# A linear attention with a mixture of four attention experts on one core: the gate logits are folded into the attention's matmul, PSUM tiles take two banks, and k^T v is computed per head on 64 columns of the array

## The chip, the cores and the metric

One core of a Trainium2 chip runs the whole program. The metric is the device time of one execution in microseconds (us), the median of several runs.

## The reference, cut to what matters

Eight batches (b) of eight heads (h), 576 tokens (s), head dimension 64; then four experts of head dimension 64 on the 512 values of each token, of which the two with the highest gate logits count.

```python
kv = np.einsum('bhsd,bhse->bhde', k, v)
out = np.einsum('bhsd,bhde->bhse', q, kv)
rms = np.sqrt(np.mean(out * out, axis=-1, keepdims=True) + 1e-06)
x = out / rms * g_norm            # then (B, S, 512)
logits = x @ w_gate               # top 2 of 4, softmax over these two
for e in range(E):
    q = x @ wq[e]
    k = x @ wk[e]
    v = x @ wv[e]
    scores = scale * (q @ k.transpose(0, 2, 1))   # causal
    a = softmax(scores)
    out += gate[e] * (a @ v @ wo[e])
```

## The kernel before

The 576 tokens are cut into five blocks (four of 128, one of 64). The program has two parts for each batch, written as Python generators. `attention` transposes q on TensorE (p_qT, L97 by way of a helper), computes k^T v for a pair of heads at a time (p_kv, L177) and keeps the two diagonal 64x64 squares of the 128x128 result (L186, L187). Then, block by block, it multiplies (p_out, L212), squares on ScalarE (sq, L220), sums on VectorE (sumsq, L222), adds eps (msq, L229), takes the power -0.5 on GpSimd (rstd, L238), scales (x_tok, L245), transposes (p_xT) and copies the result twice (xT as float32, L202, and xT_r in fp32r, L203).

`moe_block` begins with the gate logits: p_lt (L266) has four columns of weights and runs over all 576 tokens in float32, ScalarE copies it, TensorE turns it back (p_log), and VectorE makes the gate from it. Then come the values p_v (L322), the output of the batch before (`moe_final`: p_y L455, y_sb L463, output transfer L464), and for each of two pairs of experts: projections p_proj (L346, cast to qTp and kTp at L358), scores p_sc (L371, first all strips of one expert, then of the other) with an Exp (PT, L378) and a causal mask on GpSimd (L384) each, p_O (L409) with the row sums in a 65th column, its scaling on VectorE (O_sc, L418), and the transpose p_OT.

A float32 matmul leaves two records in the trace, one in fp32r or bfloat16 leaves one: p_kv has 4 pairs x 5 blocks = 20 matmuls a batch and 40 records.

While one batch is in `moe_block`, steps of the next batch's `attention` are put between its steps at a fixed ratio (`run_interleaved`). A scheduler then sets the order on each engine; the engines work off their own order without overtaking, and wait for one another by semaphores. PSUM is one pool of eight one-bank tiles. SP issues all transfers: the weights first, then q, k and v of batch 0 and 1, block by block in turn, in pieces of 256 bytes; the loads of batch b+2 are issued when batch b begins.

## Time and profile before

| | |
|---|---|
| median of 3 runs | 517.08 us (516.87 to 517.32) |
| span of the profiled execution, first to last instruction | 515.2 us |
| that span beside the median | 1.9 us shorter |
| TensorE busy, records | 400.2 us, 2472 |
| VectorE, ScalarE, GpSimd busy | 197.3, 173.9, 124.2 us |
| mean granted TensorE clock | 0.838 |

The profile gives no time of its own for the profiled execution besides the span; what lies around the span is taken as its distance from the median. Matmuls are pipelined and a record's own length is longer than its distance to the next, so costs are read from rows that span several records. The granted clock has two levels, 2.4 GHz (1.00) and 1.2 GHz (0.50); a mean between them says how much of a stretch ran at which.

### The profile page before, as it was taken

How to read it: one execution, taken by the hardware profiler on the slowest of the kernel's cores; microseconds unless marked ns; L12 is line 12 of the kernel's file. 1: busy time of each engine (PE TensorE's matmuls, PEld its weight loads, DVE VectorE, ACT ScalarE, POOL GpSimd, SP SyncE). 2: the span in 40 equal slices, each digit the busy share in tenths (PEclk: the TensorE clock that was granted, in tenths of full speed). 3: DMA queues.
4: the chain of work that ended last, by engine and by line, in shares of the span. 5: the costliest groups of instructions: out<-in, count | busy, mean ns of one | idle time of the engine just before them, and what ended most of it. 6: DMA issues, size and time to landing. Idle time of an engine off the chain costs nothing.

```text
span 515.2 us, 7111 instructions
## 1 busy us (share of the span) xinstructions
PE 400.2 (78%) x2472; PEld 285.5 (55%) x2472; DVE 197.3 (38%) x717; ACT 173.9 (34%) x569; POOL 124.2 (24%) x234
## 2 busy tenths in 40 slices
PE   0066696959969899679968799679968799679884
PEld 0055285726758467554757368454757367564661
DVE  1104334354252342543443442543433542543523
ACT  0013143611514215252246215251245215251440
POOL 3004202430132302351043302351043302340220
PEclk9999799869955599797988699796988699796866
DMA  8999908801390015900295014900200011000202
GB/s 168 206 195 204 206 13 160 118 1 42 108 205 15 2 41 128 199 2 0 92 182 96 1 41 119 207 3 0 87 7 1 1 42 52 0 2 1 93 0 92
DMA packets 125107, 40.31 MB, mean 78 GB/s; under 512 B 120208, under 2 KB 120208, under 8 KB 125072
## 3 DMA queue, kind: packets, MB, share of 16 engines
q1 hardware_dynamic: 125072, 39.87, 38.8%
q8 instruction: 19, 0.31, 0.3%
q14 instruction: 16, 0.13, 0.1%
HBM read 30.42 MB, written 9.44 MB: 77 GB/s over the span
## 4 chain that ended last, share of the span: by engine, by line
PE 56%; DVE 13%; POOL 11%; ACT 8%; issue 5%; DMA 3%; SPq 3%; POOLq 0%; DVEq 0%; ACTq 0%
POOL rstd L238 11%; PE p_kv L177 10%; PE p_lt L266 9%; PE p_proj L346 9%; PE p_out L212 5%; PE p_v L322 4%; PE p_qT L97 4%; DVE O_sc L418 4%; PE p_O L409 4%; PE p_y L455 3%; DVE x_tok L245 3%; PE p_sc L371 3%; ACT PT L378 3%; DVE sumsq L222 3%; ACT sq L220 2%
## 5 line engine op out<-in xcount | busy, mean ns | idle before, releaser
L384 POOL TENSOR_SCALAR_AFFINE_SELECT PT<-PT 128x128 bf16<-128x128 bf16 (+1 forms) x160 | 44.0, 290 | 195.4 <-ACT PT L378 191.0
L238 POOL TENSOR_TENSOR rstd<-msq,neg_half 128x8 f32<-128x8 f32 (+1 forms) x40 | 65.8, 1645 | 102.3 <-DVE msq L229 98.8
L378 ACT ACTIVATE PT<-p_sc 128x64 bf16<-128x64 f32 (+5 forms) x288 | 65.1, 341 | 14.5 <-PE p_sc L371 13.8
L409 PE MATMUL p_O<-vext,PT 128*128 128x65 bf16 (+2 forms) x480 | 43.5, 232 | 22.0 <-DVE x_tok L245 20.3
L371 PE MATMUL p_sc<-qTp,kTp 64*128 64x64 f32 (+5 forms) x288 | 49.3, 305 | 6.7 <-ACT kTp L358 4.2
L212 PE MATMUL p_out<-kv_all,qT_all 128*128 128x128 f32 (+1 forms) x320 | 52.8, 318 | 2.1 <-ACT PT L378 2.1
L245 DVE TENSOR_TENSOR x_tok<-p_out,rstd 128x512 f32<-128x512 f32 (+1 forms) x40 | 27.6, 689 | 65.3 <-POOL rstd L238 65.3
L177 PE MATMUL p_kv<-v_b,k_b 128*128 128x128 f32 (+1 forms) x320 | 51.7, 300 | 0.0
L97 PE MATMUL p_OT<-ident_b,O_sc 128*128 128x128 bf16 (+1 forms) x80 | 21.8, 273 | 38.4 <-DVE O_sc L418 38.1
L97 PE MATMUL p_qT<-ident_f,q_b 128*128 128x128 f32 (+1 forms) x160 | 28.6, 288 | 29.1 <-DMA q_b<-in_q_dram 29.1
L266 PE MATMUL p_lt<-xT,wg_f 128*4 128x64 f32 (+1 forms) x128 | 50.9, 564 | 0.0
L418 DVE TENSOR_SCALAR O_sc<-p_O,invr,gate 128x64 bf16<-128x64 f32 (+1 forms) x160 | 49.8, 334 | 1.6 <-PE p_OT L97 0.6
L409 PEld LDWEIGHTS <-PT 128*128 128x128 bf16 (+2 forms) x480 | 31.8, 124 | 30.8 <-POOL PT L384 11.1
L371 PEld LDWEIGHTS p_sc<-qTp,kTp 64*128 64x128 f32 (+1 forms) x288 | 39.3, 188 | 16.0 <-ACT kTp L358 5.8
L212 PEld LDWEIGHTS p_out<-kv_all,qT_all 128*128 128x128 f32 (+1 forms) x320 | 44.8, 209 | 5.8 <-ACT PT L378 3.5
L220 ACT ACTIVATE sq<-p_out 128x512 f32<-128x512 f32 (+1 forms) x40 | 23.8, 596 | 66.4 <-PE p_out L212 58.9
L222 DVE TENSOR_REDUCE sumsq<-sq 128x8 f32<-128x512 f32 (+1 forms) x40 | 27.2, 680 | 47.8 <-ACT sq L220 47.8
L177 PEld LDWEIGHTS p_kv<-v_b,k_b 128*128 128x128 f32 (+1 forms) x320 | 41.5, 194 | 6.3 <-issue 0.2
L174 ACT COPY qT_all<-p_qT 128x512 f32<-128x512 f32 x64 | 23.0, 419 | 61.5 <-PE p_qT L97 61.5
L186 DVE COPY kv_all<-p_kv 64x64 f32<-64x64 f32 x32 | 6.9, 216 | 90.1 <-PE p_kv L177 87.3
L97 PEld LDWEIGHTS p_qT<-ident_f,q_b 128*128 128x128 f32 (+1 forms) x160 | 19.4, 143 | 37.4 <-DMA q_b<-in_q_dram 19.9
L97 PE MATMUL p_xT<-ident_f,x_tok 128*128 128x128 f32 (+1 forms) x160 | 30.8, 330 | 8.7 <-DVE x_tok L245 5.8
(53 smaller groups left out, 419.9 us busy)
## 6 DMA issues: line engine op xcount, KB each, us to landing
q_b<-in_q_dram SPq DMA_DIRECT2D x32, 256.0 KB, 5.0
k_b<-in_k_dram SPq DMA_DIRECT2D x32, 256.0 KB, 5.0
v_b<-in_v_dram SPq DMA_DIRECT2D x32, 256.0 KB, 5.1
out_dram<-y_sb SPq DMA_DIRECT2D x32, 256.0 KB, 2.1
q_b<-in_q_dram SPq DMA_DIRECT2D x8, 128.0 KB, 5.1
k_b<-in_k_dram SPq DMA_DIRECT2D x8, 128.0 KB, 4.8
v_b<-in_v_dram SPq DMA_DIRECT2D x8, 128.0 KB, 4.4
out_dram<-y_sb SPq DMA_DIRECT2D x8, 128.0 KB, 2.3
```

The lines of the kernel that those rows point to most:

```text
L97: nc.tensor.transpose(out_ap, in_ap, ident[:npart, :npart])
L177: nc.tensor.matmul(p_kv[:, :], lhsT=kb[:nt, i, 2 * hp : 2 * hp + 2, :].rearrange("p h d -> p (h d)"), rhs=vb[:nt, i, 2 * hp : 2 * hp + 2, ...
L212: nc.tensor.matmul(p_out[:nt, hp * P : (hp + 1) * P], lhsT=qT2_all[:, hp, t0 : t0 + nt], rhs=kv2_all[:, hp, :], start=True, stop=True,)
L238: nc.gpsimd.tensor_tensor(out=rstd[:nt, :], in0=msq[:nt, :], in1=neg_half[:nt, :], op=AluOpType.pow,)
L245: nc.vector.tensor_tensor(out=x_tok[:nt, :].rearrange("p (h d) -> p h d", h=H), in0=p_out[:nt, :].rearrange("p (h d) -> p h d", h=H), in1= ...
L266: nc.tensor.matmul(p_lt[:, :], lhsT=wg_f[:, c, :], rhs=xT_sb[:, c, slo:shi], start=(c == 0), stop=(c == NCH - 1),)
L346: nc.tensor.matmul(p_proj[:, :], lhsT=wsrc[:, c, 2 * pr : 2 * pr + 2, :].rearrange("p e f -> p (e f)"), rhs=xT_r[:, c, plo:phi], start=(c ...
L371: nc.tensor.matmul(p_sc[:nk, :], lhsT=kT_pair[pb : pb + Hd, t0 : t0 + nk], rhs=qT_pair[pb : pb + Hd, lo:hi], start=True, stop=True,)
L378: nc.scalar.activation(PT[:nk, off + (lo - t0) : off + (hi - t0)], p_sc[:nk, :], ACTF.Exp, scale=scale,)
L384: nc.gpsimd.affine_select(out=PT[:nk, off : off + nk], in_=PT[:nk, off : off + nk], compare_op=AluOpType.is_ge, fill=0.0, base=0, pattern= ...
L409: nc.tensor.matmul(p_O[:nq, :], lhsT=PT[:nkk, col : col + nq], rhs=v_ext[:nkk, kbi, e, :], start=(kbi == 0), stop=(kbi == qci),)
L418: nc.vector.tensor_scalar(out=O_sc[:nq, el, :], in0=p_O[:nq, 0:Hd], scalar1=invr[:nq], scalar2=gate[:nq, qci, e : e + 1], op0=AluOpType.mu ...
```

## The change

It is a new text for nearly the whole kernel. What it does:

- The gate weights (scaled by g_norm) are multiplied with k^T v: per pair of heads one transpose (p_kt) and one matmul of 8 columns (p_kg), and the result stands as four more columns behind each head's 64 in kvx. p_out so gives the gate logits of each head unscaled; VectorE scales them with rstd (gl) and sums over heads (lg8). p_lt, its copies and p_log are gone, and so is the float32 copy of xT.
- k^T v is computed per head: 64 columns of weights, output on partitions 0 to 63 or 64 to 127, the two heads of a pair in turn. k and v come as 512 tokens with four in a row on one partition (1 KB runs); the remaining 64 tokens stand in tiles that are padded with zeros to 128 partitions. q comes as before.
- PSUM has three tiles of two banks (p_proj, p_sc, p_O, p_out) and two tiles of one bank (everything else).
- Projections are cut into 288 + 288 tokens. The scores of the two experts of a pair alternate, one bank each, and one Exp and one mask take both.
- p_O's reciprocal and scaling take three blocks and two experts at once; y is copied by ScalarE instead of VectorE; four y tiles instead of two.
- eps is a 65th column of sq, so msq is gone; q's copy moves from ScalarE to VectorE.
- Loads of batch 0 stand ahead of the weights, those of batch 1 behind them, with k and v ahead of q.
- `weave` puts the next batch's `stage1` between the steps of `stage2` by costs written beside each yield. `stage2` has both projections and scores first, then the output of the batch before, then both p_O.

```diff
...
+        step = 2 if fine else H
+        for h0 in range(0, H, step):
+            main(kt, k, h0, h0 + step)
+            main(vt, v, h0, h0 + step)
+            if h0 == 0:
+                rem(kr[b % 2], k)
+                rem(vr[b % 2], v)
+        for i, (t0, nt) in enumerate(blocks):
+            nc.sync.dma_start(
+                qt[:nt, i, :, :], q[b, :, t0 : t0 + nt, :].rearrange("h p d -> p h d")
+            )
...
+    def big(name):
+        return ps2.tile([P, 2, 512], FP32, tag="big", name=name)
+
+    def small(shape, name, dtype=FP32):
+        return ps1.tile(shape, dtype, tag="small", name=name)
...
+    loads = {0: load_qkv(0, fine=True)}
...
+    loads[1] = load_qkv(1)
...
+    def kv_pair(p_kv, c, kb, vb, krem, vrem):
+        for j in range(NF + 1):
+            for hh in range(2):
+                h = 2 * c + hh
+                lk, rv = (kb[:, h, j, :], vb[:, h, j, :]) if j < NF else (krem[:, h, :], vrem[:, h, :])
+                nc.tensor.matmul(
+                    p_kv[hh * Dh : (hh + 1) * Dh, c, :], lhsT=lk, rhs=rv,
+                    start=(j == 0), stop=(j == NF), skip_group_check=True,
+                )
+
+    def kv_copy(p_kv, kvb, kv2):
+        for hh in range(2):
+            pp = slice(hh * Dh, (hh + 1) * Dh)
+            nc.vector.tensor_copy(out=kvb[pp, :, hh, 0:Dh], in_=p_kv[pp, :, :])
+            nc.scalar.copy(kv2[pp, :, hh * Dh : (hh + 1) * Dh], p_kv[pp, :, :])
...
+        yield 4.3
...
+        p_kg = small([P, NCH, 2, E], "p_kg")
+        for c in range(NCH):
+            nc.tensor.matmul(
+                p_kg[:, c, :, :].rearrange("p a e -> p (a e)"),
+                lhsT=kt_sb[:, c, :],
+                rhs=wg_bd[:, c, :, :].rearrange("p a e -> p (a e)"),
+                start=True,
+                stop=True,
+            )
+        nc.vector.tensor_copy(out=kvb[:, :, :, Dh:GW], in_=p_kg[:])
...
+            p_o = big("p_out")
             for c in range(NCH):
...
+                    p_o[:nt, c // 2, (c % 2) * 2 * GW : (c % 2 + 1) * 2 * GW],
+                    lhsT=qT[:, c, t0 : t0 + nt],
+                    rhs=kvb[:, c, :, :].rearrange("p a g -> p (a g)"),
+                    start=True,
+                    stop=True,
+                )
+            po = p_o[:nt, :, 0 : 4 * GW].rearrange("p k (h g) -> p k h g", g=GW)
+            sq = sqs[i % 3]
+            nc.scalar.activation(
+                sq[:nt, :, 0:Dh].rearrange("p (k h) d -> p k h d", k=2),
+                po[:, :, :, 0:Dh],
+                ACTF.Square,
+                scale=1.0 / (Dh**0.5),
+            )
...
+            ms = blk.tile([P, H], FP32, tag="ms", name="ms")
+            nc.vector.tensor_reduce(ms[:nt], sq[:nt], axis=AX_X, op=AluOpType.add)
...
+            gl = blk.tile([P, H, E], FP32, tag="gl", name="gl")
+            nc.vector.tensor_tensor(
+                out=gl[:nt].rearrange("p (k h) e -> p k h e", k=2),
+                in0=po[:, :, :, Dh:GW],
+                in1=rb.to_broadcast([nt, 2, 4, E]),
+                op=AluOpType.mult,
+            )
+            nc.vector.tensor_reduce(
+                lg8[:nt, i, 0:E],
+                gl[:nt].rearrange("p h e -> p e h"),
+                axis=AX_X,
+                op=AluOpType.add,
+            )
...
+            if len(pend) > 1:
+                x_flush()
+                yield 0.45
...
+        def proj(pr):
+            out_t = []
+            for nm in ("q", "k"):
+                p_p = big("p_proj")
+                for c in range(NCH):
+                    for s in range(2):
...
+                nc.scalar.copy(
+                    t[:, 0:S].rearrange("p (s n) -> p s n", s=2), p_p[:, :, 0:HALF]
+                )
...
+            def piece(parts):
+                p_s = big("p_sc")
+                o = 0
+                for kb, lo, hi in parts:
+                    for el in range(2):
+                        pb = slice(el * Hd, (el + 1) * Hd)
...
+                            p_s[:, el, o : o + hi - lo],
...
+                    o += hi - lo
+                kb, lo, hi = parts[0]
+                d0 = strip_off[kb] + lo - kb * P
+                nc.scalar.activation(PT[:, :, d0 : d0 + o], p_s[:, :, 0:o], ACTF.Exp, scale=scale)
...
+            PT = res["PT", pr]
+            p_O = big("p_O")
...
+            groups = ((0, (0, 1, 2)), (1, (3, 4)))
+            for bank, qcs in groups:
...
+                    iv = inv[:nq, sub[0] : sub[0] + nn, :]
...
+                    nc.vector.tensor_tensor(
+                        out=osc[:nq, sub[0] : sub[0] + nn, :, :].rearrange("p n e f -> p (n e) f"),
+                        in0=po[:, :, 0:Hd],
+                        in1=iv.rearrange("p n e -> p (n e)").unsqueeze(2).to_broadcast([nq, 2 * nn, Hd]),
+                        op=AluOpType.mult,
...
+        yield from proj(0)
+        yield from scores(0)
+        yield from proj(1)
+        yield from scores(1)
+        if prev_y is not None:
+            yield from prev_y
+        yield from pv(0)
+        yield from o_t(0)
+        yield from pv(1)
+        yield from o_t(1)
...
+            y = ysb.tile([P, D], FP32, tag="y", name="y")
+            nc.scalar.copy(y[:nq, :], p_y[:nq, :])
+            nc.sync.dma_start(out[b, s0 : s0 + nq, :], y[:nq, :])
+            yield 0.45
...
+    W1, W2 = 16.0, 17.0
+
+    def weave(main, side):
+        a = s = 0.0
+        live = side is not None
+        for c in main:
+            a += c / W2
+            while live and s < a:
                 try:
...
```

The order that the scheduler makes of it shows at three places. The first is TensorE at the point where a batch's work begins. Before (`p_lt` is the gate logits, `p_kv` is k^T v of the next batch):

```order
L97 MATMUL p_OT<-ident_b,O_sc 128x64
L266 MATMUL p_lt<-xT,wg_f 4x512 x4
L266 MATMUL p_lt<-xT,wg_f 4x64 x4
L97 MATMUL p_log<-ident_f,lgT 128x4 x4
L322 MATMUL p_v<-wv_r,xT_r 128x256
L97 MATMUL p_log<-ident_f,lgT 64x4
L322 MATMUL p_v<-wv_r,xT_r 128x256 x11
L97 MATMUL p_qT<-ident_f,q_b 128x128 x4
L97 MATMUL p_qT<-ident_f,q_b 128x64
L177 MATMUL p_kv<-v_b,k_b 128x128 x5
```

Now, from the last transpose of x (`p_x`):

```order
L242 MATMUL p_x<-ident_f,x_tok 128x64 x4
L351 MATMUL p_proj<-xT,wk_r 128x288
L463 LDWEIGHTS osc
L463 MATMUL p_OT<-ident_b,osc 128x128
L333 MATMUL p_v<-wv_r,xT 128x256 x4
L351 MATMUL p_proj<-xT,wq_r 128x288 x2
L463 LDWEIGHTS osc
L463 MATMUL p_OT<-ident_b,osc 128x64
L351 MATMUL p_proj<-xT,wq_r 128x288 x3
L175 MATMUL p_kv<-v_b,k_b 64x64 x8
L175 MATMUL p_kv<-v_rem_96,k_rem_94 64x64 x2
```

The gate logits have left; values, projections and the whole k^T v of the next batch (four such groups of ten) follow the last p_x directly.

The second place is VectorE in the chain of two successive blocks of the next batch. Before:

```order
L222 TENSOR_REDUCE sumsq<-sq 128x8
L203 CAST xT_r<-xT 128x4x128
L229 SCALAR_TENSOR_TENSOR msq<-sumsq,eps_row 128x8
L245 TENSOR_TENSOR x_tok<-p_out,rstd 128x512
L222 TENSOR_REDUCE sumsq<-sq 64x8
L203 CAST xT_r<-xT 128x4x128
L229 SCALAR_TENSOR_TENSOR msq<-sumsq,eps_row 64x8
L245 TENSOR_TENSOR x_tok<-p_out,rstd 64x512
```

Now, the fourth and the fifth block (`inv`, `osc` belong to p_O, `gl` and `lg` to the gate):

```order
L273 TENSOR_TENSOR x_tok<-p_out,rstd 128x512
L280 TENSOR_TENSOR gl<-p_out,rstd 128x32
L447 TENSOR_TENSOR inv<-inv,gate 128x2
L446 RECIPROCAL inv<-p_O 128x6
L286 TENSOR_REDUCE lg_0_102<-gl 128x4
L451 TENSOR_TENSOR osc<-p_O,inv 128x128
L446 RECIPROCAL inv<-p_O 64x2
L447 TENSOR_TENSOR inv<-inv,gate 128x6
L308 MAX m_2310<-lg_0_102 128x8
L447 TENSOR_TENSOR inv<-inv,gate 64x2
L451 TENSOR_TENSOR osc<-p_O,inv 128x384
L451 TENSOR_TENSOR osc<-p_O,inv 64x128
```

Behind them follow one more MAX and then the fifth block's `ms<-sq`. A scaling still stands directly behind its own block's sum or one or two small instructions later, and p_O's instructions stand between the blocks.

The third place is VectorE at the start of the program. Before:

```order
L121 TENSOR_SCALAR wq_r<-w_stage,g_wide 128x1024
L128 TENSOR_SCALAR wg_f<-wg_f,g_wide 128x16
L140 CAST wo_pairs<-wo_f 128x1024
L121 TENSOR_SCALAR wk_r<-w_stage,g_wide 128x1024
L121 TENSOR_SCALAR wv_r<-w_stage,g_wide 128x1024
L186 COPY kv_all<-p_kv 64x64
```

Now:

```order
L201 COPY qT<-p_q 128x4x64
L155 TENSOR_SCALAR wv_r<-w_stage,g_wide 128x1024
L266 TENSOR_REDUCE ms<-sq_118 128x8
L273 TENSOR_TENSOR x_tok<-p_out,rstd 128x512
L155 TENSOR_SCALAR wq_r<-w_stage,g_wide 128x1024
L280 TENSOR_TENSOR gl<-p_out,rstd 128x32
L266 TENSOR_REDUCE ms<-sq_120 128x8
```

All weights were scaled ahead of the first copy of k^T v; the scaling of wv now stands between batch 0's last q copy and its first block's sum, that of wq between the first and the second block.

## Rows read from the trace of the kernel before

**Rows 1.** The page's head and its part 1: busy us (share of the span) xinstructions.

```profile
span 515.2 us, 7111 instructions
...
PE 400.2 (78%) x2472; PEld 285.5 (55%) x2472; DVE 197.3 (38%) x717; ACT 173.9 (34%) x569; POOL 124.2 (24%) x234
```

**Rows 2.** Chain of waits in order of time: start us, us, what.

```profile
58.58 5.29 PE p_lt L266 x8
...
300.13 1.50 PE p_v L322 x11
302.27 1.50 PE p_kv L177 x10
...
307.92 1.52 PE p_y L455 x6
309.44 1.49 PE p_proj L346 x8
...
321.86 1.65 POOL rstd L238
325.41 1.65 POOL rstd L238
...
336.28 1.10 PE p_out L212 x8
...
343.00 1.64 POOL rstd L238
347.34 1.35 PE p_O L409 x15
350.74 5.99 PE p_lt L266 x8
...
466.82 5.97 PE p_lt L266 x8
```

**Rows 3.** Stages: stretch, us; PE, PEld, DVE, ACT, POOL busy; clock, DMA share, GB/s.

```profile
292.50:300.10 7.60, 7.38 (x24) 1.99 (x23) 0.00 (x0) 0.96 (x4) 0.00 (x0) 0.66 0.01 2
300.10:318.60 18.50, 18.19 (x118) 14.26 (x118) 7.81 (x29) 6.38 (x23) 1.01 (x4) 1.00 0.22 72
318.60:350.70 32.10, 22.92 (x172) 18.25 (x172) 16.38 (x61) 14.13 (x47) 14.54 (x24) 0.81 0.66 107
```

**Rows 4.** The same chain between 318 and 335 us, in full.

```profile
319.99 0.61 ACT sq L220
...
320.62 0.69 DVE sumsq L222
...
327.08 0.70 DVE x_tok L245
```

**Rows 5.** Waits: engine line, waited for: us in total, times, longest us.

```profile
DVE x_tok L245 <- POOL rstd L238: 65.3, 40, 2.3
```

**Rows 6.** Timeline of TensorE's weight loads, second part of p_lt: start us, us.

```profile
298.46 0.42 PEld L266 LDWEIGHTS p_lt<-xT,wg_f 128*4 128x4 f32 x7 [0.34 <-issue]
```

**Rows 7.** Groups of instructions: xcount | busy us, mean ns | idle before.

```profile
L177 PE MATMUL p_kv<-v_b,k_b 128*128 128x128 f32 (+1 forms) x320 | 51.7, 300 | 0.0
...
L378 ACT ACTIVATE PT<-p_sc 128x512 bf16<-128x512 f32 x32 | 19.2, 599 | 9.4 <-PE p_sc L371 9.4
...
L378 ACT ACTIVATE PT<-p_sc 128x256 bf16<-128x256 f32 x32 | 13.1, 411 | 0.0
```

**Rows 8.** The start: chain of waits and, in the row with DMA_DIRECT2D, SP's timeline.

```profile
9.15 3.45 DMA w_stage<-in_moe_wk_dram
...
16.86 1.27 SPq L151 DMA_DIRECT2D v_b<-in_v_dram  x1
...
44.14 1.66 POOL rstd L238
...
55.37 1.69 POOL rstd L238
```

**Rows 9.** The chain's last output transfer but one, 256 KB.

```profile
509.18 2.03 DMA out_dram<-y_sb
```

More of the change, by code (lines that the diff above doesn't have):

```diff
@@ L56 @@
[L56 to L81 removed]
+    NF = S // P
@@ L83 @@
+    REM = S - NF * P
+    NB = NF + 1
+    HALF = S // 2
+    blocks = [(i * P, min(P, S - i * P)) for i in range(NB)]
+    scale = 1.0 / (Hd**0.5)
+    strip_w = [S - t0 for t0, _ in blocks]
+    strip_off = [sum(strip_w[:i]) for i in range(NB)]
+    strips = sum(strip_w)
+    GW = Dh + E
     const = ctx.enter_context(tc.tile_pool(name="const", bufs=1))
-    wts = ctx.enter_context(tc.tile_pool(name="wts", bufs=1))
+    wst = ctx.enter_context(tc.tile_pool(name="wst", bufs=2))
     qkvp = ctx.enter_context(tc.tile_pool(name="qkv", bufs=2))
-    attn = ctx.enter_context(tc.tile_pool(name="attn", bufs=2))
@@ L265, in moe_block @@
             for c in range(NCH):
                 nc.tensor.matmul(
-                    p_lt[:, :],
-                    lhsT=wg_f[:, c, :],
-                    rhs=xT_sb[:, c, slo:shi],
-                    start=(c == 0),
-                    stop=(c == NCH - 1),
-                )
-            nc.scalar.copy(lgT[:, slo:shi], p_lt[:, :])
-        p_log = psum([P, NB, E], name="p_log")
-        for i, (t0, nt) in enumerate(blocks):
-            pe_transpose(p_log[:nt, i, :], lgT[:, t0 : t0 + nt], E)
@@ new lines, in stage1 @@
+            rstd = blk.tile([P, H], FP32, tag="rstd", name="rstd")
+            nc.gpsimd.tensor_tensor(
+                out=rstd[:nt], in0=ms[:nt], in1=neg_half[:nt], op=AluOpType.pow
+            )
+            xt = blk.tile([P, D], FP32, tag="x_tok", name="x_tok")
+            rb = rstd[:nt].rearrange("p (k h) -> p k h", k=2).unsqueeze(3)
+            nc.vector.tensor_tensor(
+                out=xt[:nt].rearrange("p (k h d) -> p k h d", k=2, h=4),
+                in0=po[:, :, :, 0:Dh],
+                in1=rb.to_broadcast([nt, 2, 4, Dh]),
+                op=AluOpType.mult,
+            )
@@ L319, in moe_block @@
+        nc.vector.tensor_tensor(out=gate[:], in0=gt[:], in1=rden[:].unsqueeze(2).to_broadcast([P, NB, E]), op=AluOpType.mult)
+        vx = vexts[b % 2]
         for i, (t0, nt) in enumerate(blocks):
-            p_v = psum([P, E * Hd], name="p_v")
+            p_v = small([P, E * Hd], "p_v")
             for c in range(NCH):
@@ new lines, in o_t @@
+        def o_t(pr):
+            osc = res["osc", pr]
+            p_t = small([P, S], "p_OT", BF16)
+            for qc, (s0, nq) in enumerate(blocks):
+                nc.tensor.transpose(
+                    p_t[:, s0 : s0 + nq],
+                    osc[:nq, qc, :, :].rearrange("p e f -> p (e f)"),
+                    ident_b[:nq, :nq],
+                )
+            nc.scalar.copy(OT[:, pr, :], p_t[:])
+            yield 0.5
+        yield from proj(0)
+        yield from scores(0)
+        yield from proj(1)
@@ L454, in moe_final, with final @@
+        yield from scores(1)
[5 more added lines that the diff above has]
+        yield from o_t(1)
+        res["OT"] = OT
+    def final(b, OT):
+        for qc, (s0, nq) in enumerate(blocks):
+            p_y = small([P, D], "p_y")
             for pr in range(EP):
                 nc.tensor.matmul(
-                    p_y[:nq, :],
-                    lhsT=OT_all[:, pr, s0 : s0 + nq],
-                    rhs=wo_pairs[:, pr, :],
@@ L459, in moe_final @@
[L459 to L475 removed]
+                    p_y[:nq, :], lhsT=OT[:, pr, s0 : s0 + nq], rhs=wo_b[:, pr, :],
@@ L478, in run_interleaved @@
                 except StopIteration:
-                    side_done = True
-        if not side_done:
-            for _ in gen_side:
-                pass
-    loads = [None] * B
-    loads[0] = load_qkv(0)
-    if B > 1:
-        loads[1] = load_qkv(1)
-    res_cur = {}
-    for _ in attention(0, *loads[0], res_cur):
+                    live = False
+        if live:
+            for _ in side:
+                pass
+    res = {}
+    for _ in stage1(0, res):
         pass
-    deferred = None
+    y_gen = None
```

577 lines of the change are left out of this document (219 added, 358 removed).

## Prediction

> **What bounds the kernel now.** The page's busy line comes first [rows 1]: TensorE is busy 400.2 of 515.2 us, VectorE 197.3, ScalarE 173.9, GpSimd 124.2. A share is a mean over stages, so the chain of waits in order of time comes next [rows 2]. It repeats: p_lt, the first work of a batch, starts at 350.74 and, two batches later, at 466.82, which is 58.0 us a batch. The first p_lt starts at 58.58; the last batch takes the 48.4 us from 466.82 to the end. So the span is 58.6 + 7 periods of 58.3 in the mean + 48.4 = 515.2.
>
> The table by stage [rows 3] cuts one batch in three: the gate logits (7.6 us, TensorE only, mean granted clock 0.66), a dense stage (18.5 us, TensorE busy 18.19, clock 1.00), and 32.1 us in which TensorE is busy 22.92, at 0.81. The third is set by one chain, which the next batch's attention puts through four engines for each of five blocks: Square on ScalarE 0.61, sum on VectorE 0.69, pow on GpSimd 1.65, scaling on VectorE 0.70 [rows 2, 4]. VectorE works in order, so it stands still through the pow: 65.3 us over the 40 blocks [rows 5]. Two blocks that follow each other directly are 3.55 us apart (321.86 to 325.41), but first to last rstd of the batch takes 343.00 - 321.86 = 21.1 us, because TensorE's work for the next block stands behind p_OT, p_proj and score work.
>
> **What the change does to a batch.** I cut the new batch where the order allows it, and price each stretch by rows of before.
>
> Stretch A, from the last xT copy to the kT cast. The gate logits are gone: all 7.6 us. What stands for them is 4 transposes, 4 matmuls of 8 columns, 8 more columns in each p_out matmul and two small VectorE instructions a block. What is left is p_v, the first p_proj and the whole p_kv. p_v: 20 records at 1.50/11 = 0.136 us [rows 2], 2.7. p_proj: now 512 and 64 columns cost 1.49/4 = 0.37 us a pair [rows 2]; two halves of 288 cost at most that and at least 0.27 (two p_v records of 256 columns); I take 0.29, 8 pairs, 2.3. p_kv: today 40 records of 128 columns at 1.50/10 = 0.150 [rows 2], 6.0 us. After it there are 40 matmuls of 64 columns which, as float32, make two records each, 80. The trace has no matmuls that alternate between the two halves of the array's columns (the last block's use the first half alone), so it is bounded: the nearest row is the 64-column part of p_lt, 7 weight loads in 0.42 us [rows 6], 0.06 each, 4.8 us; above, the 0.150 of now gives 12.0; below, two tiles at once give half of 4.8, 2.4. I take 4.8. Then the kT cast of 576 columns, 0.65 (below). A begins, as p_lt does now, behind a stretch with an idle TensorE: p_lt's 7.6 us at mean clock 0.66 are (1 - 0.66)/0.5 x 7.6 = 5.2 us at the lower level, which lose half, 2.6 us; I charge the same. The first p_v and two p_proj stand ahead of the last xT copy in the order, 0.8 off. A = 2.7 + 2.3 + 4.8 + 0.65 + 2.6 - 0.8 = 12.2.
>
> First a row, then a page on it: ten p_kv records, eight on 128 rows and two on 64, take 1.50 us, where eight p_out take 1.10 [rows 2], 0.138 each, so the ten cost 0.12 more than ten of these. The Trainium skill (TensorEngine Tiling (Array Packing), Key Properties) says that a change of tiling mode drains TensorE; the new order changes mode some ten times a batch, and at an estimated 0.1 us each, from that row, this would make the sum 8 us longer. The zero-padded remainder tiles take away the changes inside p_kv, and I charge none.
>
> Stretch B, both heads' scores and the second p_proj, runs at ScalarE's pace. Exp takes 0.599 for 512 columns and 0.411 for 256 [rows 7], 0.73 ns a column; the new pieces have 576, 576, 896, 640 and 512 columns over two banks: 0.65 + 0.65 + 0.88 + 0.69 + 0.60 = 3.47 for each half. There are three two-bank tiles. The second p_proj waits for the third exp (0.35 + 2.2 after the first score), takes 1.15, then the gate matmuls 0.3, the second half 1.15, cast 0.65, first score 0.4, four exps 2.87, and Square of block 0 stands behind them, 0.61. B = 9.7. If both elements' scores run beside each other in the array, nothing changes here: exp is later.
>
> Stretch C, the chain of the five blocks with p_O around it. The eps is folded into the sum, so msq falls out: 0.69 + 0.15 (handing over) + 1.65 + 0.70 = 3.2, and with the three small instructions for the gate behind it 3.55, the pitch of today's pair. VectorE still stands behind every pow, but reciprocals and osc of p_O stand in that gap in the new order. Five blocks 17.8; between the fourth scaling and the fifth sum stand eleven instructions of p_O's, 2.2; then p_x, xT copy and handing over, 1.0. C = 21.0, against 32.1 now. The y copies go from VectorE to ScalarE, 5 x 0.6, and lie in C, where ScalarE waits anyhow; they delay Square of block 1 by 1.2, inside the pow of block 0. If that cover fails they cost up to 3.0.
>
> A period is 12.2 + 9.7 + 21.0 = 42.9, say 43, against 58.0.
>
> **Both ends.** The start: SP issues 256 KB in 256-byte pieces in 1.27 us [rows 8]. Now the weights go first, and the first p_lt starts at 58.58. After it k, v and q of batch 0 go first, 13.5 such units, 17 us; k and v come in 1 KB runs (2 KB rows of the output land 256 KB in 2.03 us [rows 9]), for which I take 4 us off, bounds 0 and 6. The sum of block 0 stands behind wv's scaling on VectorE, so it also waits for wv: two units, 2.5, and landing 3.45 [rows 8], with the small loads about 21 us. The chain then runs as today at the start, with sums ahead of scalings: first to last rstd 55.37 - 44.14 = 11.2 [rows 8], with 3.2 for the last block, two weight scalings and the last transposes 17. The start is 38, bounds 34 to 42. Loads of later batches are issued behind output transfers that wait for y, but they have two batches' time; I charge nothing, and if they come late the dense stretch waits up to 5 us.
>
> The end: the last batch has no chain beside it. A without p_kv 7, B with the fifth exp 10, y copies of the batch before 3, p_O, osc and p_OT twice 8 (p_O 1.35/15 = 0.09 a record [rows 2]), the last five y 4, landing and end 3: about 34 less overlaps, 33.5, against 48.4.
>
> Sum: 38 + 7 x 43 + 33.5 = 372.5 us of span. The profiled execution's span of 515.2 lies 1.9 below the median 517.08, and I add that: **374.4**.
>
> **Rivals.** (1) Two column tiles run at once: p_kv at 2.4 instead of 4.8 gives 2.4 x 8 = 19 less, **355**. For it: different array columns and different output partitions. Against it: no row shows it. The Trainium skill (TensorEngine Tiling (Array Packing), Key Properties) says that tiles load and multiply independently, which would be this case. (2) The chain hides and TensorE's own work is the bound: p_kv 4.8, 44 transposes at p_kv's 0.150 6.6, p_out 40 x 0.138 5.5, p_v 2.7, p_proj 4.6, scores 3, p_O 5.4, p_OT 1, p_y 10 x 0.25 2.5 is 36.1 a batch: 38 + 7 x 36.1 + 33.5 + 1.9 = **326**. Against it: the sums stand behind the scalings on VectorE in the order. (3) The chain stays loose: in-order TensorE puts p_x of one block ahead of p_out of the next, and the five rstd keep today's spacing of 21.1/4 = 5.3 instead of 3.55. That is 1.75 x 5 = 8.8 a batch: 38 + 7 x 51.8 + 34 + 1.9 = **437**. For it: it is what happens now. (4) Slower than before: the array does not pipeline column tiles, and each p_kv record takes its own full duration, 0.300 us in the mean row [rows 7], 24 us a batch instead of 4.8; 8 x 19.2 = 154 more, **528**. It decides from (517 - 374)/8/80 = 0.22 above my 0.06, that is 0.28 us a record. For it: no row shows the second half of the columns in use alone; against it: 64-row records follow each other without such a gap.
>
> **Chances.** Forecast 0.60, (1) 0.17, (2) 0.05, (3) 0.14, (4) 0.03, no difference 0.01. The range reaches down past (1) with a start and an end at their lower bounds, and up to where half of (3) would be: 338 to 412. It leaves out (2), most of (3) and (4). About 0.2% is what a measurement of this kernel can tell: faster by more 0.96, within 0.01, slower by more 0.03.
>
> **What would show it.** Right: batches some 43 us apart (p_v to p_v); rstd rows about 3.6 us apart with VectorE idle before each x_tok; first p_v at 36 to 42 us; p_kv's 80 records in about 5 us. Wrong: p_kv over 12 us, a chain in which p_x stands between two rstd, waits of p_kv for k_b, or ScalarE as the engine without gaps in B and C.

## The result and the profile after

The changed kernel takes 370.85 us (median, 370.28 to 371.19), the kernel before 516.98 beside it: a ratio of 0.718, 95% interval 0.715 to 0.721. The forecast was 374.4, range 338 to 412. Some kernels below ran in two ways, over 1.5% apart at different granted clocks (the power on VectorE: 332 and 336 us against 339 and 340), and such kernels are compared by their shorter runs.

The page's head, its busy line, the row of granted clock in 40 slices, and the shares of the chain that ended last:

```profile
span 368.6 us, 6665 instructions
...
PE 298.2 (81%) x2616; PEld 237.2 (64%) x2624; DVE 157.5 (43%) x513; ACT 152.6 (41%) x273; POOL 102.9 (28%) x146
...
PEclk9978599578999599977999689986999589986975
...
PE 46%; POOL 17%; DVE 17%; ACT 10%; issue 3%; SPq 2%; DMA 2%; POOLq 0%; ACTq 0%; DVEq 0%
```

TensorE lost 102 us against [rows 1], and 146.6 us of span went. The rest is idle time. Part of the chain of waits in order of time (start us, us, what); one batch runs from the p_v at 251.87 to the one at 294.00:

```profile
41.70 1.15 PE p_v L333 x4
...
251.87 1.01 PE p_v L333 x4
...
254.55 3.17 PE p_kv L175 x80
...
269.02 2.49 ACT PT L389 x4
...
271.56 0.61 ACT sq L259
...
272.19 0.70 DVE ms L266
...
273.03 1.65 POOL rstd L268
...
276.68 1.65 POOL rstd L268
...
280.39 1.65 POOL rstd L268
...
283.60 1.65 POOL rstd L268
...
285.27 0.69 DVE x_tok L273
...
286.11 0.41 PE p_x L242 x2
286.51 1.30 PE p_out L250 x6
...
290.17 1.64 POOL rstd L268
...
294.00 1.01 PE p_v L333 x4
...
336.09 1.01 PE p_v L333 x4
```

First p_v at 41.70, last at 336.09, the end at 368.6: 41.7 + 7 x 42.06 + 32.5. The period was 58.0 [rows 2]. The same batch by stages, cut as the prediction cut it (A, B, C), and C once more in two parts; the columns are those of [rows 3]:

```profile
251.90:262.20 10.30, 10.30 (x124) 9.18 (x126) 3.94 (x12) 2.66 (x5) 0.00 (x0) 0.80 0.01 2
262.20:272.20 10.00, 9.62 (x75) 7.62 (x75) 3.60 (x8) 7.54 (x13) 3.10 (x8) 1.00 0.01 2
272.20:294.00 21.80, 16.25 (x132) 12.06 (x132) 11.56 (x46) 8.78 (x17) 8.79 (x7) 0.83 0.16 55
...
272.20:286.10 13.90, 9.02 (x89) 6.97 (x89) 7.31 (x23) 6.51 (x12) 7.15 (x6) 1.00 0.25 85
286.10:294.00 7.90, 7.23 (x43) 5.09 (x44) 4.25 (x25) 2.27 (x5) 1.63 (x1) 0.54 0.01 2
```

A is TensorE's own (10.30 of 10.30 us busy). In B TensorE is busy for 9.62 of 10.00 us, but the chain leaves it at the second half's first scores and goes over four Exp (269.02) and Square. C is the chain: TensorE has work for 16.25 of 21.80 us. The first four rstd are 3.65, 3.71 and 3.21 us apart, the fifth 6.57: TensorE, working in order, has the fourth block's p_x ahead of the last p_out. C's last 7.9 us ran at a mean clock of 0.54. VectorE's wait for the power is still there, 54.9 us against 65.3 in [rows 5]:

```profile
DVE x_tok L273 <- POOL rstd L268: 54.9, 39, 1.8
```

So the theory at this point was: two column tiles overlap, which makes A short; C is set by the latency of the chain, with pow as its longest part; the start waits for the gate weights. The experiments below test it.

### The profile page after: what moved, and what is told of

It reads as the page before. It is cut to its first block, busy times and chain, and to the rows that moved or that the text cites. A ratio compares the mean times of both kernels' runs of the same rounds, so it can differ in the third digit from the quotient of the medians.

```text
span 368.6 us, 6665 instructions
## 1 busy us (share of the span) xinstructions
PE 298.2 (81%) x2616; PEld 237.2 (64%) x2624; DVE 157.5 (43%) x513; ACT 152.6 (41%) x273; POOL 102.9 (28%) x146
## 4 chain that ended last, share of the span: by engine, by line
PE 46%; POOL 17%; DVE 17%; ACT 10%; issue 3%; SPq 2%; DMA 2%; POOLq 0%; ACTq 0%; DVEq 0%
POOL rstd L268 17%; PE p_proj L351 11%; PE p_v L333 7%; ACT PT L389 7%; DVE x_tok L273 7%; DVE ms L266 7%; PE p_kv L175 6%; PE p_out L250 5%; PE p_q L196 4%; PE p_sc L379 3%; PE p_x L242 2%; ACT sq L259 2%; PE p_kg L220 2%; SPq L130 2%; PE p_O L431 2%
## 5 line engine op out<-in xcount | busy, mean ns | idle before, releaser
L268 POOL TENSOR_TENSOR rstd<-ms,neg_half 128x8 f32<-128x8 f32 (+1 forms) x40 | 65.4, 1637 | 101.4 <-DVE ms L266 70.1
L394 POOL TENSOR_SCALAR_AFFINE_SELECT PT<-PT 128x256 bf16<-128x256 bf16 (+1 forms) x80 | 30.0, 385 | 148.8 <-ACT PT L389 148.1
L242 PE MATMUL p_x<-ident_f,x_tok 128*128 128x128 f32 (+1 forms) x160 | 30.7, 318 | 41.4 <-DVE gl L280 35.4
L250 PE MATMUL p_out<-kvx,qT 128*128 128x136 f32 (+1 forms) x320 | 55.1, 315 | 2.1 <-DVE inv L447 0.7
L389 ACT ACTIVATE PT<-p_sc 128x576 bf16<-128x576 f32 (+3 forms) x80 | 50.3, 712 | 7.2 <-PE p_sc L379 7.1
L250 PEld LDWEIGHTS p_out<-kvx,qT 128*128 128x128 f32 (+1 forms) x320 | 44.8, 197 | 11.5 <-issue 3.3
L273 DVE TENSOR_TENSOR x_tok<-p_out,rstd 128x512 f32<-128x512 f32 (+1 forms) x40 | 27.6, 690 | 55.0 <-POOL rstd L268 54.9
L266 DVE TENSOR_REDUCE ms<-sq 128x8 f32<-128x520 f32 (+1 forms) x40 | 27.2, 680 | 26.9 <-ACT sq L259 26.9
L333 PE MATMUL p_v<-wv_r,xT 128*128 128x256 f32 (+1 forms) x160 | 31.7, 335 | 0.3 <-DVE vext L340 0.3
L351 PE MATMUL p_proj<-xT,wq_r 128*128 128x288 f32 x128 | 31.4, 367 | 0.3 <-ACT PT L389 0.3
L379 PE MATMUL p_sc<-qTp,kT 64*128 64x288 f32 (+2 forms) x192 | 27.3, 345 | 2.0 <-ACT PT L389 1.7
```

The source lines that it names most:

```text
L242: nc.tensor.transpose(p_x[:, c, :nt], xt[:nt, c * P : (c + 1) * P], ident_f[:nt, :nt])
L250: nc.tensor.matmul(p_o[:nt, c // 2, (c % 2) * 2 * GW : (c % 2 + 1) * 2 * GW], lhsT=qT[:, c, t0 : t0 + nt], rhs=kvb[:, c, :, :].rearrange(" ...
L266: nc.vector.tensor_reduce(ms[:nt], sq[:nt], axis=AX_X, op=AluOpType.add)
L268: nc.gpsimd.tensor_tensor(out=rstd[:nt], in0=ms[:nt], in1=neg_half[:nt], op=AluOpType.pow)
L273: nc.vector.tensor_tensor(out=xt[:nt].rearrange("p (k h d) -> p k h d", k=2, h=4), in0=po[:, :, :, 0:Dh], in1=rb.to_broadcast([nt, 2, 4, Dh]),
L333: nc.tensor.matmul(p_v[:nt, :], lhsT=xT[:, c, t0 : t0 + nt], rhs=w_r["v"][:, c, :, :].rearrange("p e f -> p (e f)"), start=(c == 0), stop= ...
```

## The experiments

**k^T v, half after half.**

```diff
-        for j in range(NF + 1):
-            for hh in range(2):
+        for hh in range(2):
+            for j in range(NF + 1):
```

> The changed kernel, but k^T v takes all five matmuls of a pair's first head and then all five of the second, instead of the two heads in turn. Theory, two column tiles in turn run at the same time: the 80 p_kv records of a batch took 2.65 us (0.033 each); one tile at a time they take what the prediction charged, 0.06 each or 4.8 us, so the distance from batch to batch goes from 42.1 to about 44.2 and the time from 370.9 to about 387. Rival, the short records come from the half width alone: 2.65 us as before, time 370 to 372.

Measured 381.3 us (381.0 to 381.6). Rows of the chain, of the changed kernel and then of this one; one p_kv of a batch is 80 records in both:

```profile
85.11 4.03 PE p_kv L175 x80
...
296.67 2.64 PE p_kv L175 x80
```

```profile
218.30 5.18 PE p_kv L175 x80
...
262.19 3.94 PE p_kv L175 x80
```

The two rows are the longest and the shortest batch of each. All of them stand partly at the lower clock: the shortest of the changed kernel has a mean of 0.75 in its first 0.63 us, that of this run 0.57 in its first 1.01. Divided by 80 they give no price at one clock. The timeline of TensorE does, where the clock is 1.00; first the changed kernel, then this run (`v_b` is the first 512 tokens of a head, eight records, `v_rem` the rest, two):

```profile
297.39 0.63 PE L175 MATMUL p_kv<-v_b,k_b 128*64 128x64 f32 x16
297.86 0.28 PE L175 MATMUL p_kv<-v_rem,k_rem 128*64 128x64 f32 x4
297.98 0.63 PE L175 MATMUL p_kv<-v_b,k_b 128*64 128x64 f32 x16
```

```profile
263.43 0.22 PE L175 MATMUL p_kv<-v_rem,k_rem 128*64 128x64 f32 x1
263.49 0.22 PE L175 MATMUL p_kv<-v_b,k_b 128*64 128x64 f32 x1
263.49 0.22 PE L175 MATMUL p_kv<-v_rem,k_rem 128*64 128x64 f32 x1
...
263.84 0.22 PE L175 MATMUL p_kv<-v_rem,k_rem 128*64 128x64 f32 x1
```

In the changed kernel twenty records, a pair of heads, take 0.58 us (297.39 to 297.98): in the trace two records, one of each head, start 3 to 4 ns apart, and the next two 58 ns later. In this run the records of one head are 58 ns apart as well (the two `v_rem` at 263.43 and 263.49), but beside the second of them the next head's `v_b` has already started: at each change of head three of ten records run beside the other head's, and ten records take 0.40 us (263.43 to 263.84). So one tile costs 0.058 a record, as the prediction charged, and two tiles in turn run at the same time, at twice the rate. The order head after head keeps three tenths of that, which is why the theory's 387 us was not reached: at a clock of 1.00 a batch's p_kv is 0.9 us longer (4 x 0.81 against 4 x 0.58), not 2.2. With the lower clock's part it is 1.4 longer, in the mean of the six batches whose 80 records stand in one row (4.67 against 3.24). Ten of the 10.5 us are 7 periods of 43.56 instead of 42.06. The rival, that the short records come from the half width alone, falls.

**k^T v for a pair of heads.**

```diff
-                nc.tensor.matmul(
-                    p_kv[hh * Dh : (hh + 1) * Dh, c, :], lhsT=lk, rhs=rv,
-                    start=(j == 0), stop=(j == NF), skip_group_check=True,
-                )
+            nc.tensor.matmul(
+                p_kv[:, c, :], lhsT=lk, rhs=rv, start=(j == 0), stop=(j == NF),
+            )
...
```

> The changed kernel, but k^T v is computed for a pair of heads at once on all 128 columns, as in the kernel before (20 matmuls and 40 records a batch, only the two diagonal squares copied); k and v are loaded in 256-byte pieces for it, four transfers each. Theory, the column tiles save what their records show: 40 records at 0.11 to 0.15 are 4.4 to 6.0 us against 2.65, so 1.8 to 3.4 us more a batch and 385 to 398 us. Rival, a change between whole array and column tiles costs a stop that is gone here, about 1 us a batch each way: 0.8 to 2.4 more a batch, 377 to 390. Rival, k^T v is covered by the copies around it: 370 to 373.

Measured 400.9 us (400.1 to 402.4). The 40 records of a batch take between these two:

```profile
146.37 6.41 PE p_kv L172 x40
...
326.52 5.14 PE p_kv L172 x40
```

The shortest is 2.5 us longer (5.14 against 2.64), both partly at the lower clock; where the clock is 1.00, ten records take 1.12 us (four times 1.12 against four times 0.58, 2.1 us more). The time overshot the first theory: the first p_v of a batch stands at 51.11 instead of 41.70, because batch 0 now comes in 256-byte pieces, and the first period is long as well (47.4 from 51.11 to 98.48): TensorE waits for v 12.1 us in all, against 5.7. The late ones, 44.4 from 323.85 to 368.27, are 2.4 longer than 42.06 and agree with the records. No gain shows from having no changes between whole array and half; one of some tenths of a microsecond a batch could be hidden in this comparison.

**The gate logits' own matmul, put back.**

```diff
+        for lo, hi in ((0, 512), (512, S)):
+            p_lt = small([E, 512], "p_lt")
+            for c in range(NCH):
+                nc.tensor.matmul(
+                    p_lt[:, 0 : hi - lo],
+                    lhsT=wg_st[:, c, :], rhs=xT[:, c, lo:hi].bitcast(FP32),
+                    start=(c == 0), stop=(c == NCH - 1),
+                )
```

> The changed kernel with the gate logits' matmul of the kernel before put back ahead of p_v: four columns of weights, all 576 tokens, float32 on xT. Nobody reads its result. Theory, the stretch A is TensorE's own (busy 10.30 of 10.30 us) and nothing covers this matmul: with the 7.6 us that it took in the kernel before, 8 times, 425 to 432. Rival, the clock: it is a long dense stretch that stands where the granted clock was 0.80, and what follows it runs at the upper level: 3.8 us a batch at the upper level less 2.6 of clock loss, 378 to 385.

Measured 403.0 us (402.5 to 407.1), 32 more, which neither range has. (This run, the pairs and the gate weights' loads were taken together, and there the kernel before took 516 to 523 us, so a difference of one per cent to other runs says nothing.) Stretch A of one batch, the logits and what follows them:

```profile
180.10:186.60 6.50, 6.50 (x19) 1.28 (x18) 0.64 (x4) 0.64 (x1) 0.00 (x0) 0.63 0.00 0
186.60:194.30 7.70, 7.70 (x120) 7.32 (x120) 2.97 (x7) 1.70 (x4) 0.00 (x0) 1.00 0.44 137
```

6.5 us of logits cost 14.2 - 10.3 = 3.9 us in this batch, and 4.4 in the mean period: they take over the time at the lower clock that p_v and p_kv have without them (0.80 in A; here 0.63 and then 1.00). The rival was right in kind, but too low with 1.2 us a batch. The 7.6 us of [rows 3] were not all the matmul's own price. The run put back the matmul alone: the copy and p_log that stood behind it in the kernel before are in the 7.6 and not in the 3.9.

**No power.**

```diff
-                out=rstd[:nt], in0=ms[:nt], in1=neg_half[:nt], op=AluOpType.pow
+                out=rstd[:nt], in0=ms[:nt], in1=neg_half[:nt], op=AluOpType.mult
```

> The changed kernel with the power -0.5 on GpSimd replaced by a multiplication of the same two operands, so that the scaling by the root mean square is left out. Theory, the chain ms, pow, x_tok sets the stretch C (21.8 us a batch, TensorE busy 16.25): with 1 us less in each of five links C falls by about 4 us, to 17 to 18, where TensorE's own work is; 8 times with the start's chain: 335 to 342. Rival, C is set by the order of TensorE's instructions (p_x of a block ahead of the p_out of the next) and the chain only follows: at most 1 us a batch, 362 to 368.

The run leaves out the scaling by the root mean square. Measured 307.0 us (306.2 to 307.7), further down than the theory said. The group of the power in the changed kernel, and here (instructions; busy us, mean ns; idle before):

```profile
L268 POOL TENSOR_TENSOR rstd<-ms,neg_half 128x8 f32<-128x8 f32 (+1 forms) x40 | 65.4, 1637 | 101.4 <-DVE ms L266 70.1
```

```profile
L268 POOL TENSOR_TENSOR rstd<-ms,neg_half 128x8 f32<-128x8 f32 (+1 forms) x40 | 8.0, 200 | 105.1 <-DVE ms L266 69.0 <-DVE inv L447 17.0 <-DVE lg L286 13.7
```

And the stages of one batch here:

```profile
103.80:113.90 10.10, 10.09 (x124) 8.99 (x126) 4.20 (x13) 2.77 (x6) 0.00 (x0) 0.83 0.99 200
113.90:123.90 10.00, 9.67 (x75) 7.62 (x74) 3.63 (x7) 7.52 (x13) 3.09 (x8) 1.00 0.49 138
123.90:138.60 14.70, 13.45 (x132) 10.30 (x130) 11.34 (x45) 8.54 (x17) 1.60 (x7) 1.00 0.65 162
```

A and B stay in this batch, C goes from 21.8 to 14.7: 7.1 us for five links of 1.44. It is one of the longer batches (34.8 us); every second one takes 33.4, with p_kv at 2.48 instead of 2.92. In the mean the period is 33.8 against 42.06, and seven of these differences are 58 of the 64 us. TensorE's work did not stop it at 16.25, because that number itself held time at the lower clock; with the gaps gone the clock is 1.00 and the same instructions are 13.45 us.

**Exp for each expert apart.**

```diff
-                nc.scalar.activation(PT[:, :, d0 : d0 + o], p_s[:, :, 0:o], ACTF.Exp, scale=scale)
+                for el in range(2):
+                    nc.scalar.activation(PT[:, el, d0 : d0 + o], p_s[:, el, 0:o], ACTF.Exp, scale=scale)
```

> The changed kernel, but the Exp of the two experts of a pair is issued apart, so 10 more ScalarE instructions a batch. Theory, the stretch B of the scores is paced by ScalarE: a fixed part of 0.22 us each (twice 411 ns for 256 elements less 599 ns for 512) makes 2.2 us more a batch and 384 to 389 us. Rival, B is set by TensorE (busy 9.62 of 10.0 us, ScalarE 7.54): 0 to 0.5 us a batch, 370 to 375.

Measured 374.6 us (373.6 to 375.5), 3.8 more. The group of Exp, changed kernel and this one:

```profile
L389 ACT ACTIVATE PT<-p_sc 128x576 bf16<-128x576 f32 (+3 forms) x80 | 50.3, 712 | 7.2 <-PE p_sc L379 7.1
```

```profile
L390 ACT ACTIVATE PT<-p_sc 128x288 bf16<-128x288 f32 (+3 forms) x160 | 56.1, 481 | 7.3 <-PE p_sc L379 7.3
```

Busy time rose by 5.8 us for 80 more instructions, 0.07 each and not 0.22: in a row they overlap. The time is in the rival's range, and the theory falls. In the chain of one batch the second half's eight Exp take 2.62 us where four took 2.49 (269.02 above), and Square 0.69 for 0.61:

```profile
229.40 2.62 ACT PT L390 x8
```

That is 0.2 us a batch. The period rose by 0.5 (42.56 against 42.06); the mean of p_kv's rows with 80 records, 2.48 at a clock of 1.00, is 3.69 us against 3.24, so the rest is stretch A with more time at the lower clock. Why there is more of it is not shown.

**Blocks in pairs.**

```diff
...
+        for a in range(0, NB, 2):
+            two = range(a, min(a + 2, NB))
+            for i in two:
+                front(i)
             yield 0.9
...
+            for _ in two:
+                finish()
                 yield 0.45
...
```

`front` holds p_out, sq, ms and rstd of a block, `finish` its x_tok, gl and lg8.

> The changed kernel with the five blocks of the chain taken two and two and one: p_out, sq, ms and pow of two blocks are written ahead of x_tok, gl and lg8 of both, so that one block's pow runs beside the other's work. Theory, the chain's latency sets stretch C: a pair costs 0.69 + 2 x 1.65 + 0.70 and hand-overs, about 5.0 us against two links of 3.6, so about 2.1 us less per pair, 4.2 a batch, and the start's chain as well: 333 to 342. Rival, two blocks hold two of the three two-bank tiles, and scores or p_O wait for the third: the gain is given back, 362 to 375.

Measured 368.0 us (365.0 to 370.6), a ratio of 0.7055 (0.698 to 0.713) to the kernel before: next to no gain. One batch's C in two parts:

```profile
187.40:199.80 12.40, 7.12 (x64) 4.85 (x63) 6.92 (x19) 5.85 (x11) 7.15 (x6) 0.98 0.66 173
199.80:210.90 11.10, 10.38 (x68) 7.71 (x68) 5.18 (x28) 2.85 (x6) 1.63 (x1) 0.50 0.01 1
```

Four blocks do take less (12.4 against 13.9), but TensorE stands idle for 5.3 us in them: its timeline shows p_O waiting 3.03 and 2.21 us for inv and osc, which stand behind the blocks' instructions on VectorE. All of TensorE's work that is left then runs at 0.50, 11.1 us against 7.9. The rival's place (p_O) was right; its cause, a lack of two-bank tiles, is not shown: these waits end with VectorE.

**Pairs with a smaller weave factor.**

```diff
-    W1, W2 = 16.0, 17.0
+    W1, W2 = 14.0, 17.0
```

> The blocks in pairs and the gate weights' loads first, and the weave's factor for the next batch's steps 14 instead of 16, so that they come earlier beside the scores. Theory, the chain then begins before TensorE has finished the scores and less of it is left uncovered: 2 us a batch less than with the pairs alone, 320 to 335. Rival, the scores need two of the three two-bank tiles, and pairs of blocks beside them stop ScalarE's row of Exp: slower than with the pairs alone.

Measured 398.5 us (396.3 to 402.1), the rival's side, but the run does not test the theory, because the edit does the opposite of what was meant. `weave` adds a step's cost divided by W1 to `s` and takes the next batch's steps as long as `s` is below `a`; a smaller W1 lets `s` grow faster, and the steps come later. The trace has it so: the first p_out stands 19.8 us behind the batch's first p_v (197.61 and 177.78), in the run with pairs alone 18.3 (185.44 and 167.18). In the batch from 177.78 to 223.93 the fifth block's p_out waits on TensorE behind p_O, p_OT and a p_x, and its last six records start at 217.75; its ms, pow and x_tok are then uncovered. The rival's reason does not show either: the five Exp of each half stand in a row of 3.09 us, as they do in the first half with pairs alone. Whether a larger W1 would gain anything was not run.

**The gate weights' loads first.**

```diff
-    loads = {0: load_qkv(0, fine=True)}
-
     g_wide = const.tile([P, 1], FP32, name="g_wide")
...
     nc.sync.dma_start(wg_st[:], moe_w_gate.rearrange("(c p) e -> p c e", p=P))
+    loads = {0: load_qkv(0, fine=True)}
+
```

> The changed kernel with the loads of g_norm and of the gate weights issued ahead of those of batch 0 instead of behind them. Theory, the first p_kg waited 1.44 us for the gate weights and everything of the start stands behind it: 1.4 us off, 369 to 370. Rival, three more issues ahead of k and v push these by about 1 us and the start stays as it is: 370.5 to 372.

Measured 372.6 us (371.6 to 374.1), ratio 0.717 (0.712 to 0.723): no difference. The first p_kg no longer waits for them, but the loads of k and v are issued 1.9 us later, and Square of block 0 starts at 25.76 instead of 24.58. So what the wait was worth stood against later loads, and this run does not part the two. Between the arrival of the data and ms of block 0 the changed kernel shows

```profile
11.50:25.20 13.70, 9.94 (x68) 8.88 (x69) 6.18 (x15) 2.61 (x4) 0.00 (x0) 0.75 0.77 142
```

which is 9.94 us of k^T v, transposes, p_kg and the first p_out at a mean clock of 0.75, with copies and waits between them. The clock is not what holds the start up: in the run with the fill below, this stretch is at 1.00 and block 0's rstd starts 1.1 us later still (27.11 against 25.99).

**The power on VectorE.** A first estimate from the number's bits, then two refinements:

```diff
-            nc.gpsimd.tensor_tensor(
-                out=rstd[:nt], in0=ms[:nt], in1=neg_half[:nt], op=AluOpType.pow
-            )
...
+            nc.vector.tensor_scalar(
+                out=yi[:nt], in0=ms[:nt].bitcast(mybir.dt.int32), scalar1=-0.5,
+                scalar2=1597463007.0, op0=AluOpType.mult, op1=AluOpType.add,
+            )
+            y = yi[:nt].bitcast(FP32)
+            for last in (False, True):
...
+                nc.vector.tensor_tensor(out=a[:nt], in0=y, in1=y, op=AluOpType.mult)
+                nc.vector.scalar_tensor_tensor(
+                    out=a[:nt], in0=a[:nt], scalar=-0.5, in1=ms[:nt],
+                    op0=AluOpType.mult, op1=AluOpType.mult,
+                )
+                nc.vector.scalar_tensor_tensor(
+                    out=rstd[:nt], in0=a[:nt], scalar=1.5, in1=y,
+                    op0=AluOpType.add, op1=AluOpType.mult,
+                )
+                y = rstd[:nt]
```

> The changed kernel with the power -0.5 computed on VectorE: one instruction that makes a first estimate from the bits of the number, then two rounds of three instructions that refine it. Seven small VectorE instructions at about 0.15 us (inv and gate of 128x6 took 0.154) are 1.05 us in place of pow's 1.65 and 0.15 of hand-overs to GpSimd and back. Theory, the latency of the link sets the time: 0.75 us less in each of 40 links is 30, and by the run with a multiplication in place of pow (1.44 us less a link gave 64 us) 33: 336 to 342. Rival, VectorE's order: instructions of p_O and of the neighbouring block stand between the seven and stretch the link to what it was: 358 to 372.

Measured 337.7 us (332.4 to 340.0), ratio 0.654 (0.649 to 0.659). The first link and the start of the second in the chain, and B and C of that batch:

```profile
208.43 0.70 DVE ms L266
...
210.73 0.69 DVE x_tok L288
...
211.52 0.60 DVE ms L266
```

```profile
198.50:208.40 9.90, 9.55 (x74) 7.54 (x74) 3.54 (x7) 7.50 (x13) 3.10 (x8) 1.00 0.51 138
208.40:225.50 17.10, 13.68 (x133) 10.48 (x133) 15.57 (x79) 8.79 (x17) 0.65 (x2) 1.00 0.50 129
```

From ms to x_tok it is 2.30 us instead of 2.5, from ms to the next ms 3.09 instead of 3.67. The link got only 0.6 shorter, the seven instructions being 0.17 to 0.24 each; C got 4.7 shorter: five times 0.6 is 3.0, and in the rest the clock has its part, which stays at 1.00 where C's last 7.9 us ran at 0.54. The theory's time was right (its shorter runs, 332.4 and 336.4, lie at and below the lower end), its price per link too large: 40 links of 0.6 are 24 us of the 33, and the clock made up for it.

**The same with two steps of the start.** The gate weights' loads between v and q, and a one-element Exp ahead of everything.

> The same, and two steps of the start: the loads of g_norm and of the gate weights stand behind those of k and v of batch 0 and ahead of q, and ScalarE loads its table by a one-element Exp before the first data are there (1.28 us of the start's chain stood there, between the two copies of kv). Theory, the start is a chain of loads, k^T v, copies and TensorE at the lower clock, so both come off: 1.3 to 2 us less than without them. Rival, the gate weights' later arrival was hidden and the table load is next to another wait: no difference.

Measured 335.2 us (332.4 to 340.1), lowest runs 332.4 in both: not told apart. The trace kept of this version is of a run of 337.7, that of the version without the two steps of one of 332.4, so their ends can't be compared; the start can in part. The steps did what they were meant to up to block 0, whose Square starts at 21.88 instead of 25.35: p_kg waits for no gate weights, and the table load stands at 0.80. What was gained is gone behind it: TensorE is at a mean clock of 0.71 from 25 to 40 us (0.96 without the steps), eight p_out take 1.83 us for 1.08, and the chain's first p_v stands at 40.88, 39.63 without the steps. The clock's share in this is not shown apart from the rest.

**TensorE kept busy in the gaps.**

```diff
             p_x = small([P, NCH, P], "p_x")
+            for _ in range(5):
+                nc.tensor.matmul(
+                    p_x[:].rearrange("p c t -> p (c t)"), lhsT=ident_b[:],
+                    rhs=fill[:], start=True, stop=True,
+                )
```

> The changed kernel with work added: five matmuls of zeros, bfloat16, 512 columns, into p_x ahead of each block's four transposes, where TensorE waits for VectorE; nothing of their result stays. Theory, part of what the chain costs is the clock that its gaps cost: the last 7.9 us of stretch C ran at 0.54 with TensorE busy 7.23, stretch A at 0.80. With the gaps filled both run at the upper level, about 3.3 and 2 us less a batch, against 1 to 2 us that the added 5.3 us lengthen: 340 to 357. Rival, the clock does not follow the gaps, or what it gives is less than the added work takes: 375 to 405.

Measured 360.8 us (360.1 to 361.7): more work, 10 us less time. A, B and C of one batch:

```profile
248.60:256.70 8.10, 8.10 (x123) 7.52 (x123) 3.30 (x8) 2.38 (x5) 0.00 (x0) 1.00 0.01 2
256.70:266.80 10.10, 9.76 (x74) 7.76 (x76) 3.74 (x7) 7.49 (x13) 3.09 (x8) 1.00 0.01 2
266.80:288.90 22.10, 18.77 (x156) 12.59 (x158) 12.77 (x49) 9.24 (x19) 8.78 (x7) 1.00 0.16 55
```

The clock is 1.00 throughout. A falls from 10.3 to 8.1, with the same work in it (p_kv 2.48 us); that is the gain. C stays (22.1): there the chain decides. Its last distance between two rstd shrinks from 6.57 to 4.33, the one before it grows from 3.21 to 4.62, and from the last rstd to the next batch's p_v it is 4.9 us instead of 3.8, with a fill of its own in that stretch. The start is 2.6 us longer (first p_v at 44.26); 1.1 of it stand ahead of the first fill, and why is not shown.

**The fill and the power on VectorE together.**

> The same fill in the kernel with the power on VectorE, whose stretch C is at 1.00 already. Theory, only the 0.83 of stretch A is left to gain, about 1.5 us a batch, and the added work stands partly on the path: 333 to 345, no better than without it. Rival, the start and the clock's rise at each batch gain more than that: 320 to 330.

Measured 329.3 us (328.5 to 331.3), ratio 0.638 (0.635 to 0.641): the fastest version that computes the reference. That is in the rival's range, and 4 us under the theory's; the version without the fill took 332.4 and 336.4 in its shorter runs. In one batch of each its C is 18.6 us against 17.1, its A 8.3 against 9.9, so what the fill gives in A it nearly takes back in C: the mean period is 37.05 against 37.28. The start is 0.9 shorter and the end 1.2. All later batches take 37.1 us, without the fill 35.3 to 38.9.

## Why the prediction was right, step by step

| term | predicted | measured |
|---|---|---|
| A | 12.2 | 10.3 |
| B | 9.7 | 10.0 |
| C | 21.0 | 21.8 |
| period (7) | 43 | 42.06 |
| start | 38 | 41.7 |
| end | 33.5 | 32.5 |
| around the span | 1.9 | 2.25 |

The last row is the median less the span of the profiled execution, which itself took 370.28 us. Seven periods are 6.6 us below the sum, the start 3.7 above, the end 1.0 below, the rest 0.35 above: 3.55 us together. That the sum came so near is luck in part. With p_kv at two tiles at once the sum would have been rival (1)'s 355, 16 us too low; with the start right as well it would have been 359, and with the start alone put right 378. The miss in p_kv stands against those in the start, C and B.

- **Removing the logits** was taken as "all 7.6 us" with 2.6 of clock loss charged back on A. Put back, the matmul alone costs 3.9 to 4.4; 7.6 less 2.6 is 5.0. The clock's price was in the sum, and the run with the gaps filled gives it a size: 2.2 us in A.
- **p_kv** is the term that was mis-sized: 4.8 us against 2.48 where the clock is 1.00 (the runs with the logits and with the fill), and 2.64 to 4.03 in the changed kernel with its share of the lower clock. The price of one tile was right (0.058 a record measured, 0.06 charged). The step that failed is the choice among the bounds: the forecast let the two tiles run one after the other, and they run at once, which is rival (1), given 0.17, in mechanism and size (2.4). The Trainium skill (TensorEngine Tiling (Array Packing), Key Properties) says that tiles load and multiply independently; the trace agrees, with one record of each tile every 58 ns. Rival (1)'s 355 was not reached, since the start was longer, and A, B and C are each 0.3 to 0.8 longer than its sum has them (A 9.8 with p_kv at 2.4). Rival (4) was excluded by the same rows.
- **Mode changes** were charged at nothing. A came out below its sum, and the run with whole-array p_kv shows no gain from the absence of those around p_kv. No run measures one alone.
- **B** had the right size for a partly wrong reason. It does not run at ScalarE's pace from end to end: TensorE sets it up to the second half's scores, then four Exp and Square do. Splitting every Exp added 0.2 us a batch there.
- **C** was right in mechanism: pitch 3.65, 3.71 and 3.21 against 3.55, VectorE waiting 1.4 us of pow's 1.64 in the mean (54.9 us in 39 waits). The step that failed is the last link. The prediction put eleven of p_O's VectorE instructions, 2.2 us, between the fourth and the fifth block; in the trace these end at 287.52, and VectorE then waits 1.82 us for Square. What sets the distance is p_x ahead of the last p_out on TensorE, 3.0 us (6.57 less 3.55): TensorE stands idle for 2.11 us until the fourth x_tok is there, and the eight p_out behind it take 1.96 us at the lower clock, 1.07 in the fastest version at 1.00. That is rival (3)'s mechanism at one of the four distances between five blocks; rival (3) charged five.
- **The start**: ms of block 0 was put at 21 us, behind wv's scaling, and stands at 25.2. The scaling ends at 24.16, and ms waits 1.05 us longer, for Square. The estimate had no term for k^T v, copies, p_kg and p_out between the data and Square; a wait of 1.44 us for the gate weights and a table load of 1.28 are among them, and with neither of the two, in the run with two steps of the start, Square came 3.5 us earlier. Which of the rest sets the start stays open. The chain behind it took 16.5 against 17.

## What to carry to other kernels

Where a chain over several engines sets a stage, shorten the slowest link itself before reordering around it: one small instruction a block on GpSimd, 40 in all, was worth 64 us of 371, and pairing the blocks next to nothing. Read the granted clock of the stage behind a stage with gaps: the price of idle time on TensorE is paid there, and work that seems removable may only have been paying it. Where two column tiles take turns, price the pair by one tile's records: 40 of 0.058 us and not 80. Before a factor in a scheduler is turned, work out which way it moves the steps, and look for it in the trace.
